# A scheduler's DMA model, the pace of attention against the FFN, and the place of one load in a fused attention and FFN kernel

## The chip, the core and the metric

The kernel runs on one core of a Trainium2 chip. Its time is the device time of one execution in microseconds (us). The core has a matrix engine (PE, whose weight loads are listed as PEld), a vector engine (DVE), a scalar engine (ACT), a general engine (POOL) and a queue engine (SP). DMAs are issued from SP and from POOL, on a queue each, and their bytes go through 16 DMA engines that both share.

## What is computed

```python
scores = scale * np.matmul(q, k.transpose(0, 1, 3, 2))     # q, k, v: 8 x 12 x 448 x 64
scores = np.einsum('bhij,hg->bgij', scores, w_pre)          # w_pre, w_post: 12 x 12
attn = np.exp(scores - np.max(scores, axis=-1, keepdims=True))
attn = attn / (np.sum(attn, axis=-1, keepdims=True) + 1e-09)
attn = np.einsum('bhij,hg->bgij', attn, w_post)
x = np.matmul(attn, v).transpose(0, 2, 1, 3).reshape(3584, 768)
h = np.maximum(x @ w_in, 0.0)                               # w_in: 768 x 2048
out = (h * h) @ w_out                                       # w_out: 2048 x 768
```

This is attention in which the 12 heads are mixed before and after the softmax ("talking heads"), and behind it an FFN with a squared ReLU.

## The kernel before

**The work of one batch.** There are eight batches. For each, T (L491, `tr`) turns q and k on PE into `qkt`; a head pair is a unit, and a batch has six. QK (L544, `qk`) makes the scores of 120 query rows and one head pair, in four row tiles of six pairs; the scores are copied to `stage` by ACT or DVE (`sev`). One DMA on SP's queue, called a move here (`rel`, L591), then lays ten query rows of all twelve heads from `stage` into a slot of `dring` (12 slots), so that heads stand on the partitions: 45 such chunks to a batch, 360 in all. `pre` (L619) mixes the heads of a chunk with one matmul, ACT takes the exponentials and their sums (L627), DVE the reciprocal (L637), POOL folds it into the second mixing matrix (`wk2s`, L643), and `post` (L675, four matmuls) mixes again. The result is copied to `a2t` (`a2ev`). AV (L737) multiplies it by v into `xt`, F1 (L796) makes 16 tiles of h, which ACT or DVE rectifies (L824, L825) and POOL squares (L834; DVE in the last batch), and F2 (L878) makes the output, which POOL's queue stores (L924).

**What has to wait for what.** A `pre` waits for its move. A move waits for all six copies of its row tile, and for the `pre` of twelve chunks earlier, whose slot it takes. AV of a half of a batch waits for its 23 or 22 chunks. F1 of a batch waits for AV of that part, and F2 of a batch for all its squares; F1 of the next batch comes behind F2 of this one. The loads are issued on POOL's queue: q and k of batch b + 1 when the last T of batch b is done, v of batch b + 1 when the last AV of batch b is done. At the start q and k of batch 0 come first, then the four pieces of `w_in`, then v of batch 0, q and k of batch 1, and `w_out`.

**The order.** All engines run a fixed order that a planner in Python (`_Plan`) writes when the kernel is built. It keeps a clock for each engine with assumed durations. PE's work is in seven streams (T, QK, pre, post, AV, F1, F2), each in its own order; `_pick` takes the next unit from the head of one of them. Among the heads that it believes ready with a margin to spare (`MARGIN`, and `MARGIN_DMA` for a `pre`, which waits for a move) it takes the one of the lowest priority number: AV 1, post 2, pre 3, QK 4, T 5, F1 and F2 5.5 to 7. The copies of ACT and DVE (`FLEX`) go to the engine that is free first by its clocks. When a DMA lands is assumed in `_commit`: loads queue behind each other (`load_free`) at the rate `LOAD`; a move that starts while loads are under way is itself delayed, and moves the end of the loads still to be issued by 500 ns. The planner only writes the order; on the chip each engine waits by semaphores for the real events.

F1 of a batch is done for all 448 columns at once, but in the batches in `split` part by part (four parts in batch 0, two halves in others).

Of the kernel before, what the change touches and what calls it, by code (L numbers as in the profile page):

```python
# [18 lines left out]
MODE_SWITCH = 100.0  # L19
ACT_BIAS = 50.0  # L20
MARGIN = 250.0
MARGIN_DMA = 1200.0
INF = float("inf")


class _Sem:
    __slots__ = ("handle", "count", "name")

    def __init__(self, handle, name):
        self.handle = handle  # L30
        self.count = 0
        self.name = name
# [31 lines left out]
class _Unit:  # L64


    __slots__ = ("prio", "mode", "nbanks", "needs", "go", "dma", "hold")

    def __init__(self, prio, go, needs, nbanks=0, mode=None, dma=False, hold=False):
        self.prio = prio  # L70
        self.go = go
        self.needs = needs
        self.nbanks = nbanks
        self.mode = mode
        self.dma = dma
        self.hold = hold


class _Plan:

    def __init__(self, nbanks):
        self.tasks = []
        self.ready = []
        self.free = {e: 0.0 for e in ENGINE_NAMES}
        self.per_engine = {e: [] for e in ENGINE_NAMES}
        self.committed = []
        self.streams = []
        self.mode = None
        self.load_free = 0.0
        self.move_free = 0.0  # L90
        self.bank_users = {i: [] for i in range(nbanks)}
        self.bank_age = {i: i for i in range(nbanks)}
        self.taken = set()
        self.age = nbanks

    def add(self, name, engine, fn, deps=(), cost=None, prio=0.0, sem=None, seminc=0,
            mode=None, after=(), dma=None):
# [21 lines left out]
    def _commit(self, t, e, start):  # L119
        t.engine = e  # L120
        held, lat = t.cost[e]
        self.free[e] = start + held
        t.end = start + lat
        if t.dma:
            kind, service = t.dma
            if kind == "load":
                self.load_free = max(self.load_free, start + 1200.0) + service
                t.end = max(start + held, self.load_free) + 1600.0
            else:
                at = start + 900.0  # L130
                behind = self.load_free - at
                if behind > 0:
                    at += min(behind, 2600.0)
                    service += 600.0
                    self.load_free += 500.0
                self.move_free = max(self.move_free, at) + service
                t.end = self.move_free + 2100.0
        t.done = True
        self.per_engine[e].append(t)
        self.committed.append(t)  # L140
        for s in t.succs:
            s.nwait -= 1
# [36 lines left out]
    def _pick(self):  # L179


        now = self.free[PE]
        found = []
        for s in self.streams:
            u = s[0] if s else None
            if u is None:
                continue
            needs = u.needs()
            if needs is None:
                continue  # L190
# [12 lines left out]
        if not found:  # L203
            return None
        first = min(f[0] for f in found)
        sure = [f for f in found if f[1] <= first + 1.0]
        if sure:
            def rank(f):
                u = f[2]
                p = u.prio  # L210
                if u.mode is not None:
                    if u.mode == self.mode:
                        p = min(p, 0.5)
                    elif u.hold and self.free_banks(first) < 4:
                        p += 10.0
                return (p, f[0])
            f = min(sure, key=rank)
        else:
            f = min(found, key=lambda f: (f[0], f[2].prio))
        return f  # L220
# [30 lines left out]
def bass_talking_heads_attention__then__ffn_squared_relu_kernel(  # L251
# [10 lines left out]
    B, H, S, D = q.shape  # L262
# [16 lines left out]
    NG = B * NCH  # L279
    scale = 1.0 / math.sqrt(D)  # L280

    with ExitStack() as es:
# [9 lines left out]
        NOS = 3  # L292
        NH1 = 3
        NWP = 4
        WC = 256
        ident = sb("ident", [128, 128], DT.bfloat16)
        mask = sb("mask", [NR, CH], DT.float32)
# [32 lines left out]
        sem_v = Sm("dv")  # L330
# [4 lines left out]
        plan = _Plan(NB)  # L335
# [73 lines left out]
        def rows(t, b, h0, nh):  # L409
            return bass.AP(t, (b * H + h0) * S * D, [[RJ * D, JB], [S * D, nh], [1, RJ * D]])  # L410

        LOAD = 1.0 / 350.0
        qk_tasks = {}
        v_of = {}

        def emit_load_qk(b):
            step = 4 if b == 0 else H
            for h0 in range(0, H, step):
                sem = sem_qk[h0 // step]

                def fn(eng, en, b=b, h0=h0, step=step, sem=sem):
                    eng.dma_start(qraw[:, h0:h0 + step, :, :],  # L422
                                  rows(q.tensor, b, h0, step)).then_inc(sem.handle, 16)
                    eng.dma_start(kraw[:, h0:h0 + step, :, :],
                                  rows(k.tensor, b, h0, step)).then_inc(sem.handle, 16)

                t = plan.add("ldqk%d_%d" % (b, h0), POOL, fn, [last.get("T")],
                             {POOL: (1400.0 if b == 0 else 2000.0, 0.0)},
                             -1e7 + h0 if b == 0 else b * 1000.0 - 1500.0, sem, 32,
                             dma=("load", 2 * step * S * D * 4 * LOAD))  # L430
                for h in range(h0, h0 + step):
                    qk_tasks[(b, h)] = t
            last["ldqk"] = t

        def emit_load_v(b):
            def fn(eng, en, b=b):
                eng.dma_start(vraw[:, :, :, :], rows(v.tensor, b, 0, H)).then_inc(
                    sem_v.handle, 16)

            last["v"] = v_of[b] = plan.add(  # L440
                "ldv%d" % b, POOL, fn, [last.get("AV")], {POOL: (1000.0, 0.0)},
                -1e5 if b == 0 else b * 1000.0 - 1600.0, sem_v, 16,
                dma=("load", H * S * D * 4 * LOAD))

        def emit_load_w(i, after=()):
# [160 lines left out]
        def unit_pre(g):  # L606
            b, c = divmod(g, NCH)
# [43 lines left out]
                    rel_wait.remove(g + NDS)  # L651
                    emit_rel(g + NDS)

            return _Unit(3.0, go, needs, 1, dma=True)

        av_of = {}

        def unit_post(g):
# [36 lines left out]
                a2_of[g] = t_a2  # L695
                give([bank], [t_a2])

            return _Unit(2.0, go, needs, 1)

        FIRST = ((0, 13), (13, HC[0]), (HC[0], 34), (34, NCH))  # L700

# [5 lines left out]

        xtev = {}
        f1_of = {}
        split = (0, B - 1)  # L710

        def unit_AV(b, part):
            half = 0 if part[0] < HC[0] else 1
# [221 lines left out]
        for b in range(B):  # L935
# [11 lines left out]
            for tile in tiles_of(b):  # L947
                for hh in range(2):
                    s_F2 += units_F2(b, tile, hh)

        emit_load_qk(0)
        emit_load_w(0)
        emit_load_v(0)
# [95 lines left out]
```

## Time and profile before

| | |
|---|---|
| median of 3 runs | 644.42 us (638.36 to 649.12) |
| profiled execution | 646.08 us, of which 644.3 us are the span of its instructions |
| mean granted PE clock | 0.957 |
| PE | busy 586.8 us (91%), 5864 matmuls |
| ACT, DVE, POOL | busy 450.4, 341.4, 311.2 us |
| moves (SP's queue) | 360, 38.56 MB |
| loads, stores (POOL's queue) | 33.82 MB |

The page lists busy time and idle time by engine and by groups of instructions, and the chain of work that ended last: from the last instruction back, at each step to what released it. Its rows name a line of the kernel and the tiles written and read (`out<-in`). Other views give the same by stretches of time, waits by pairs, and a timeline.

### The profile page before, as it was taken

What the parts mean: (1) busy time and instruction counts of PE and PEld (TensorE: products, weight loads), DVE (VectorE), ACT (ScalarE), POOL (GpSimd) and SP (SyncE); (2) the same over time, 40 slices, a digit from 0 to 9 for tenths busy, and PEclk for the clock granted to TensorE, in tenths of its full rate; (3) what the DMA queues carried; (4) which work ended last, traced back from release to release, by engine and by line L of the source; (5) the groups of instructions that cost most, each with busy time, mean ns of one, the idle gap of its engine ahead of it and who ended that gap; (6) DMA issues with size and microseconds to landing.
All of it is one profiled execution on the core that took longest, in us unless ns stands there. A gap on an engine that the chain in (4) does not pass through costs nothing.

```text
span 644.3 us, 15422 instructions
## 1 busy us (share of the span) xinstructions
PE 586.8 (91%) x5864; PEld 381.9 (59%) x5864; DVE 341.4 (53%) x854; ACT 450.4 (70%) x1163; POOL 311.2 (48%) x634
## 2 busy tenths in 40 slices
PE   4584999997999898979997999999999999999995
PEld 3243778665566555536654376655765476656973
DVE  3362988675677576643776337870674557300410
ACT  2571987995888787757887578965898688652531
POOL 8831768334483534545436444537446534571001
PEclk9775999998999999979999899999999999999998
DMA  9999959849752974482738636450635455301002
GB/s 138 217 229 170 172 120 167 157 113 152 131 115 51 177 164 115 84 166 44 154 83 146 120 40 153 108 145 5 117 97 117 89 104 127 94 1 48 28 25 73
DMA packets 95180, 73.36 MB, mean 114 GB/s; under 512 B 5508, under 2 KB 93060, under 8 KB 95108
## 3 DMA queue, kind: packets, MB, share of 16 engines
q0 software_dynamic: 48256, 33.82, 32.9%
q1 hardware_dynamic: 46852, 38.56, 25.9%
q8 instruction: 47, 0.77, 0.5%
q14 instruction: 25, 0.20, 0.1%
HBM read 45.62 MB, written 11.01 MB: 88 GB/s over the span
## 4 chain that ended last, share of the span: by engine, by line
PE 76%; DMA 16%; POOL 2%; SPq 2%; ACT 1%; DVE 1%; issue 1%; POOLq 0%; ACTq 0%
PE ps L878 21%; PE ps L796 20%; PE ps L675 11%; DMA dring<-stage 9%; PE ps L619 9%; DMA kraw<-in_k_dram 7%; PE ps L737 6%; PE ps L544 6%; PE ps L491 3%; SPq L591 2%; DVE stage L353 1%; POOL h2t L834 1%; POOL qraw L422 1%; POOL wk2s L643 1%; ACT stage L352 0%
## 5 line engine op out<-in xcount | busy, mean ns | idle before, releaser
L627 ACT ACTIVATE pring<-ps 120x448 bf16<-120x448 f32 x360 | 192.5, 554 | 38.2 <-PE ps L619 36.9
L643 POOL TENSOR_SCALAR wk2s<-wk2b,rinv 120x120 bf16<-120x120 bf16 x360 | 128.7, 364 | 142.4 <-DVE rinv L637 140.3
L353 DVE CAST a2t<-ps 112x480 bf16<-112x480 f32 x215 | 136.7, 649 | 87.9 <-PE ps L675 86.7
L878 PE MATMUL ps<-w_out_sb,h2t 128*128 128x384 bf16 x896 | 170.8, 326 | 0.0
L796 PE MATMUL ps<-xt,w_in_sb 128*128 128x448 bf16 (+6 forms) x1152 | 170.1, 294 | 0.0
L619 PE MATMUL ps<-dring,wk 120*120 120x448 bf16 x360 | 118.8, 372 | 25.5 <-DMA dring<-stage 24.8
L834 POOL TENSOR_TENSOR h2t<-h1t 128x448 bf16<-128x448 bf16 (+4 forms) x160 | 112.0, 707 | 53.2 <-ACT h1t L824 20.7
L796 PEld LDWEIGHTS ps<-xt,w_in_sb 128*128 128x128 bf16 x1152 | 95.0, 99 | 54.2 <-issue 8.4
L675 PE MATMUL ps<-wk2s,pring 120*128 120x120 bf16 x1440 | 121.2, 221 | 2.0 <-ACT stage L352 0.9
L675 PEld LDWEIGHTS ps<-wk2s,pring 120*128 120x128 bf16 x1440 | 95.6, 100 | 40.9 <-issue 9.4
L353 DVE CAST stage<-ps 120x896 bf16<-120x896 f32 (+1 forms) x95 | 102.2, 1084 | 26.9 <-PE ps L544 25.6
L878 PEld LDWEIGHTS ps<-w_out_sb,h2t 128*128 128x128 bf16 x896 | 83.9, 98 | 54.4 <-issue 4.7
L352 ACT ACTIVATE stage<-ps 120x896 bf16<-120x896 f32 (+1 forms) x97 | 86.2, 917 | 23.1 <-PE ps L544 21.8
L352 ACT ACTIVATE a2t<-ps 112x480 bf16<-112x480 f32 x145 | 80.8, 573 | 21.0 <-PE ps L675 20.0
L824 ACT ACTIVATE h1t<-ps 128x448 bf16<-128x448 f32 (+6 forms) x121 | 53.3, 445 | 40.7 <-PE ps L796 39.4
L637 DVE RECIPROCAL rinv<-rowsum 120x1 f32<-120x1 f32 x360 | 52.0, 155 | 54.7 <-ACT pring L627 53.5
L627 ACT ACTIVATION_READ_ACCUMULATOR pring<-ps 120x1 f32 x360 | 78.1, 217 | 0.0
L924 POOL DMA_DIRECT2D out_dram<-osb x56 | 30.5, 546 | 86.3 <-ACT osb L352 62.3
L619 PEld LDWEIGHTS ps<-dring,wk 120*120 120x120 bf16 x360 | 45.6, 137 | 44.0 <-DMA dring<-stage 14.0
L544 PE MATMUL ps<-qkt 64*120 64x448 bf16 (+1 forms) x384 | 60.3, 385 | 2.8 <-DVE stage L353 2.0
L825 DVE TENSOR_SCALAR h1t<-ps 128x448 bf16<-128x448 f32 (+5 forms) x71 | 28.8, 410 | 60.6 <-PE ps L796 57.7
L737 PE MATMUL ps<-a2t,vraw 112*64 112x230 bf16 (+5 forms) x864 | 41.6, 257 | 0.6 <-DVE rinv L637 0.6
(31 smaller groups left out, 272.4 us busy)
## 6 DMA issues: line engine op xcount, KB each, us to landing
dring<-stage SPq DMA_DIRECT2D x352, 105.0 KB
vraw<-in_v_dram POOLq DMA_DIRECT2D x8, 672.0 KB, 8.0
qraw<-in_q_dram POOLq DMA_DIRECT2D x7, 672.0 KB, 11.8
kraw<-in_k_dram POOLq DMA_DIRECT2D x7, 672.0 KB, 17.2
w_in_sb<-in_moe_w_in_dram POOLq DMA_DIRECT2D x8, 384.0 KB, 13.0
w_out_sb<-in_moe_w_out_dram POOLq DMA_DIRECT2D x12, 256.0 KB, 42.4
out_dram<-osb POOLq DMA_DIRECT2D x8, 336.0 KB, 3.7
out_dram<-osb POOLq DMA_DIRECT2D x8, 288.0 KB, 2.8
```

The source lines that it names most:

```text
L352: return eng.activation(o, i_, AF.Copy)
L353: return eng.tensor_copy(o, i_)
L544: r_ = eng.matmul(ps[0:nr, banks[par], 0:S], qkt[r0:r0 + 64, pb, p, 0, T * IT:T * IT + nr], qkt[r0:r0 + 64, pb, p, 1, :], start=True, stop ...
L619: return eng.matmul(ps[0:NR, bank, 0:S], wk1[:, :, :], dring[:, slot, :], start=True, stop=True)
L627: return eng.activation(pring[:, pr, 0:S], ps[0:NR, bank, 0:S], AF.Exp, accum_out=rowsum[:, pr, :])
L643: return eng.tensor_scalar(wk2s[:, ws, :], wk2b[:, :, :].rearrange("p a b -> p (a b)"), rinv[:, pr, :], 1.0, op0=ALU.mult, op1=ALU.mult)
L675: r_ = eng.matmul(ps[0:128, bank, jb * NR:(jb + 1) * NR], pring[:, pr, jb * JB:jb * JB + 128], wk2s[:, ws, :], start=True, stop=True,)
L737: r_ = eng.matmul(ps[kk * 64:kk * 64 + 64, bank, x * n:(x + 1) * n], vraw[:, h, r, :], a2t[half][:, r, h, a0:a0 + n], start=(r == 0), stop ...
L796: r_ = eng.matmul(ps[:, bank, 0:n], w_in_sb[:, ft, t16 * 128:(t16 + 1) * 128], xt[:, ft, c0:c1], start=(ft == 0), stop=(ft == NFT - 1),)
L824: return eng.activation(h1t[:, s, 0:n], ps[:, bank, 0:n], AF.Relu)
L834: return eng.tensor_tensor(h2t[:, t16, o0:o0 + n], h1t[:, s, 0:n], h1t[:, s, 0:n], ALU.mult)
L878: r_ = eng.matmul(ps[:, bank, 0:FH], h2t[:, t16, col:col + 128], w_out_sb[:, t16, hh * FH:(hh + 1) * FH], start=(t16 == 0), stop=(t16 == N ...
```

## The change

It has six edits, all in what the planner assumes or is told; no engine instruction has another shape but those of F1 of batch 1.

1. A move that is issued while loads are under way now delays every load that is not yet believed landed, by 520 ns (`STEAL`), and not only loads still to come.
2. The assumed rate of the loads is 385 and not 350 bytes a nanosecond.
3. A `pre` is believed sure only when its move is expected to have landed 3 us earlier (`MARGIN_DMA`), before 1.2 us.
4. `ahead` holds attention back: when more than 60 chunks plus the share of the FFN already done (times 360) have been posted, `pre` and `post` get 5 added to their priority number, and come behind T and F1, and level with F2 or behind it.
5. v of batch 0 is issued behind the first piece of `w_in` and not behind the fourth.
6. F1 of batch 1 is done in two halves.

```diff
-MARGIN_DMA = 1200.0
+MARGIN_DMA = 3000.0
+STEAL = 520.0
...
@@ _Plan._commit
             if kind == "load":
                 self.load_free = max(self.load_free, start + 1200.0) + service
                 t.end = max(start + held, self.load_free) + 1600.0
+                self.loads.append(t)
             else:
                 at = start + 900.0
                 behind = self.load_free - at
                 if behind > 0:
                     at += min(behind, 2600.0)
                     service += 600.0
-                    self.load_free += 500.0
+                    self.load_free += STEAL
+                    self.loads = [x for x in self.loads if x.end > max(at, self.move_free)]
+                    for x in self.loads:
+                        x.end += STEAL
                 self.move_free = max(self.move_free, at) + service
                 t.end = self.move_free + 2100.0
...
@@ _Plan._pick
         if sure:
+            late = self.ahead()
+
             def rank(f):
                 u = f[2]
                 p = u.prio
+                if late and u.paced:
+                    p += 5.0
...
-        LOAD = 1.0 / 350.0
+        LOAD = 1.0 / 385.0
...
@@ emit_load_v (VPOS = 0.5)
-                -1e5 if b == 0 else b * 1000.0 - 1600.0, sem_v, 16,
+                -2e5 + VPOS if b == 0 else b * 1000.0 - 1600.0, sem_v, 16,
...
-            return _Unit(3.0, go, needs, 1, dma=True)
+            return _Unit(3.0, go, needs, 1, dma=True, paced=True)
...
-            return _Unit(2.0, go, needs, 1)
+            return _Unit(2.0, go, needs, 1, paced=True)
...
-        split = (0, B - 1)
+        split = (0, 1, B - 1)
...
+        f_all = [len(s_F1), len(s_F2)]
+
+        def ahead():
+            done = (f_all[0] - len(s_F1)) / f_all[0] + (f_all[1] - len(s_F2)) / f_all[1]
+            return NG - len(s_post) > LEAD + NG * done / 2
+
+        plan.ahead = ahead
```

The lines of the changed kernel are numbered 15 higher in this part: T is L506, QK L559, `pre` L634, `post` L690, AV L752, F1 L811, F2 L893.

**The first place is on PE, near the start**, where T of batch 1 (the rows with `ident`) stands. Before, it comes behind three tiles of F1 of the first part of batch 0 (130 columns, six matmuls a tile):

```order
L675 MATMUL ps<-wk2s,pring 128x120 x12
L619 MATMUL ps<-dring,wk 120x448
L675 MATMUL ps<-wk2s,pring 128x120 x4
L796 MATMUL ps<-xt,w_in_sb 128x130 x12
L619 MATMUL ps<-dring,wk 120x448
L796 MATMUL ps<-xt,w_in_sb 128x130 x6
L491 MATMUL ps<-ident,qraw 64x112 x8
L491 MATMUL ps<-ident,kraw 64x112 x8
```

In the changed kernel the same place goes on with F1, QK, `pre` and `post` of batch 0; its T of batch 1 comes only behind these rows, the last of a stretch that begins at the same `pre`:

```order
L634 MATMUL ps<-dring,wk 120x448 x4
L690 MATMUL ps<-wk2s,pring 128x120 x4
L634 MATMUL ps<-dring,wk 120x448
L752 MATMUL ps<-a2t,vraw 64x100 x48
L690 MATMUL ps<-wk2s,pring 128x120 x20
L811 MATMUL ps<-xt,w_in_sb 128x100 x21
L690 MATMUL ps<-wk2s,pring 128x120 x4
L811 MATMUL ps<-xt,w_in_sb 128x100 x3
L506 MATMUL ps<-ident,qraw 64x112 x8
L506 MATMUL ps<-ident,kraw 64x112 x8
```

Between that `pre` (chunk 18 of batch 0) and T of batch 1 there stood 6 matmuls of F1 (of the 18 shown, 12 stand ahead of the `pre`); now there are 96 of 130 columns and 24 of 100, 12 of QK, 12 `pre`, 56 of `post` and 48 of AV.

**The second place is on PE, where batch 2 begins.** Before, the last rows of T of batch 3 (which let POOL issue the loads of q and k of batch 4) stand two rows above this piece, and the second matmul of the row `x2` that ends it is `pre` of chunk 5 of batch 2:

```order
L878 MATMUL ps<-w_out_sb,h2t 128x384 x4
L675 MATMUL ps<-wk2s,pring 128x120 x4
L619 MATMUL ps<-dring,wk 120x448
L544 MATMUL ps<-qkt 120x448 x2
L619 MATMUL ps<-dring,wk 120x448 x2
L878 MATMUL ps<-w_out_sb,h2t 128x384 x4
L675 MATMUL ps<-wk2s,pring 128x120 x8
L619 MATMUL ps<-dring,wk 120x448
L675 MATMUL ps<-wk2s,pring 128x120 x4
L619 MATMUL ps<-dring,wk 120x448
L878 MATMUL ps<-w_out_sb,h2t 128x384 x4
L619 MATMUL ps<-dring,wk 120x448 x2
```

In the changed kernel T of batch 3 is followed by chunks 24 and on of batch 1, six `pre` in a row among them:

```order
L506 MATMUL ps<-ident,qraw 64x112 x8
L506 MATMUL ps<-ident,kraw 64x112 x8
L690 MATMUL ps<-wk2s,pring 128x120 x8
L634 MATMUL ps<-dring,wk 120x448 x6
L893 MATMUL ps<-w_out_sb,h2t 128x384 x8
L690 MATMUL ps<-wk2s,pring 128x120 x4
L634 MATMUL ps<-dring,wk 120x448
L690 MATMUL ps<-wk2s,pring 128x120 x4
L634 MATMUL ps<-dring,wk 120x448
```

T of batch 3 has moved ahead by some 16 chunks, and the loads that it releases with it; F1 of batch 1 stands between it and batch 2.

**The third place is on POOL, at the start**, with the queue of loads. Before:

```order
L459 DMA w_in_sb<-in_moe_w_in_dram 128x6x256 x2
L377 AFFINE_SELECT mask<-mask 120x10
L459 DMA w_in_sb<-in_moe_w_in_dram 128x6x256 x4
L437 DMA vraw<-in_v_dram 112x12x256
L422 DMA qraw<-in_q_dram 112x12x256
```

In the changed kernel:

```order
L452 DMA vraw<-in_v_dram 112x12x256
L392 AFFINE_SELECT mask<-mask 120x10
L474 DMA w_in_sb<-in_moe_w_in_dram 128x6x256 x6
L437 DMA qraw<-in_q_dram 112x12x256
L439 DMA kraw<-in_k_dram 112x12x256
```

v has passed three pieces of `w_in` (six DMAs); what comes behind it is as before.

More of the change, by code (lines that the diff above doesn't have):

```diff
@@ L64, with __init__ @@
 class _Unit:
-    __slots__ = ("prio", "mode", "nbanks", "needs", "go", "dma", "hold")
-    def __init__(self, prio, go, needs, nbanks=0, mode=None, dma=False, hold=False):
+    __slots__ = ("prio", "mode", "nbanks", "needs", "go", "dma", "hold", "paced")
+    def __init__(self, prio, go, needs, nbanks=0, mode=None, dma=False, hold=False,
+                 paced=False):
+        self.paced = paced
         self.prio = prio
@@ L90, in __init__ @@
         self.move_free = 0.0
+        self.loads = []
         self.bank_users = {i: [] for i in range(nbanks)}
@@ L94, in __init__ @@
         self.age = nbanks
+        self.ahead = lambda: False
     def add(self, name, engine, fn, deps=(), cost=None, prio=0.0, sem=None, seminc=0,
@@ L294, in bass_talking_heads_attention__then__ffn_squared_relu_kernel @@
         NWP = 4
+        LEAD = 60
+        VPOS = 0.5
         WC = 256
```

## The prediction

> **What bounds the kernel now.** I read the page first: the busy shares, the slices in time and the granted clock.
>
> ```profile
> PE 586.8 (91%) x5864; PEld 381.9 (59%) x5864; DVE 341.4 (53%) x854; ACT 450.4 (70%) x1163; POOL 311.2 (48%) x634
> PE   4584999997999898979997999999999999999995
> PEclk9775999998999999979999899999999999999998
> PE 76%; DMA 16%; POOL 2%; SPq 2%; ACT 1%; DVE 1%; issue 1%; POOLq 0%; ACTq 0%
> ```
>
> PE is the bound: it is busy 586.8 of 644.3 us, and idle 57.5 us. A 9 in its slices is 90% or more, so the idle time sits in the first four slices (16 us each) and in a few dents in the middle; the granted clock drops in the same slices. In the chain of work that ended last, DMAs hold 16%. The waits of PE say which:
>
> ```profile
> PE ps L619 <- DMA dring<-stage: 24.8, 18, 4.9
> PE ps L491 <- DMA kraw<-in_k_dram: 11.5, 2, 10.7
> PE ps L491 <- POOL ident L363: 8.2, 1, 8.2
> ```
>
> Columns: us in total, times, the longest. `pre` waits for moves, and T for the load of k, once for 10.7 us. The third row is the start of the program, which nothing here touches; these three are 44.5 of the 57.5 us, and 7 more are the last store. Then the busy time by stretches (us, busy time of PE, PEld, DVE, ACT, POOL with their instructions, then the granted clock, the DMA engines' share and GB/s):
>
> ```profile
> 19.40:46.90 27.50, 19.50 (x167) 11.46 (x165) 13.52 (x36) 18.01 (x50) 13.67 (x29) 0.69 1.35 226
> 46.90:57.80 10.90, 0.21 (x6) 0.07 (x4) 0.46 (x2) 0.51 (x2) 1.77 (x5) 0.65 1.19 203
> 57.80:63.80 6.00, 6.00 (x106) 5.68 (x107) 3.51 (x6) 1.50 (x3) 0.89 (x1) 0.50 0.92 125
> 63.80:140.00 76.20, 75.23 (x1131) 56.36 (x1130) 60.98 (x170) 66.77 (x193) 46.98 (x129) 1.00 0.82 146
> 140.00:360.00 220.00, 200.39 (x1949) 124.73 (x1948) 133.94 (x325) 169.79 (x443) 106.30 (x215) 0.96 0.64 123
> 360.00:560.00 200.00, 198.76 (x1793) 123.83 (x1792) 112.09 (x273) 156.94 (x402) 101.82 (x199) 1.00 0.45 99
> 560.00:637.30 77.30, 77.25 (x606) 53.60 (x603) 9.20 (x33) 29.41 (x67) 22.34 (x30) 1.00 0.12 37
> ```
>
> Two places are worth anything: the 10.7 us before T of batch 1 (46.9 to 57.8), and 19.6 us (220.00 less 200.39) between 140 and 360. From 360 to the last matmul PE idles 1.3 us in 277; the last 77 us are F1 and F2 alone, and PE fills them. The chain in order of time shows what the waits in the middle are (start, us, what):
>
> ```profile
> 16.95 40.68 DMA kraw<-in_k_dram
> 148.49 8.29 DMA dring<-stage
> 268.67 9.52 DMA dring<-stage
> 347.13 8.31 DMA dring<-stage
> 494.66 3.90 DMA dring<-stage
> ```
>
> A move takes 3.9 us from issue to landing when it runs alone (the row at 494.66) and 8.3 to 9.5 us in the three that held PE up. What ran beside them is on POOL's timeline:
>
> ```profile
> 148.23 1.00 POOL L422 DMA_DIRECT2D qraw<-in_q_dram  x1
> 149.23 0.95 POOL L424 DMA_DIRECT2D kraw<-in_k_dram  x1
> ```
>
> The load of q and k goes out at 148.23, the move that PE will wait for at 148.49. So the stalls are collisions: a row tile's moves start together with a load, and the `pre` that needs them stands too close behind.
>
> **The start.** k of batch 1 is issued at 16.95 and lands at 57.63. PE comes to T at 46.9, with nothing else in its order. The new order puts a block in between, from the counts under the first order rows:
>
> ```profile
> L796 PE MATMUL ps<-xt,w_in_sb 128*128 128x130 bf16 x96 | 7.4, 220 | 0.0
> L796 PE MATMUL ps<-xt,w_in_sb 128*128 128x100 bf16 x96 | 6.0, 208 | 0.0
> L544 PE MATMUL ps<-qkt 64*88 64x448 bf16 x96 | 15.2, 371 | 0.0
> L737 PE MATMUL ps<-a2t,vraw 112*64 112x100 bf16 x48 | 1.3, 208 | 0.0
> 304.90 1.37 PE ps L675 x24
> 306.27 1.14 PE ps L619 x6
> ```
>
> Matmuls overlap, so a price is busy time by count and not the mean: 96 of F1 at 130 columns 7.4 us; 24 at 100 columns a quarter of 6.0, 1.5; 12 of QK an eighth of 15.2, 1.9; 48 of AV 1.3; 56 of `post` at 57 ns (1.37 by 24) 3.2; 12 `pre` at 0.19 (1.14 by 6) 2.3. That is 17.6 us. From 46.6 (the end of the `pre` of chunk 18, 0.3 us ahead of the stall) PE comes to T at 64.2, behind the landing at 57.63. So the wait of 10.7 us should go; what is late next is the copies. They are 12 exponentials with the reading of their sum, 14 copies to `a2t`, 6 to `stage` and 20 ReLUs:
>
> ```profile
> L627 ACT ACTIVATE pring<-ps 120x448 bf16<-120x448 f32 x360 | 192.5, 554 | 38.2 <-PE ps L619 36.9
> L627 ACT ACTIVATION_READ_ACCUMULATOR pring<-ps 120x1 f32 x360 | 78.1, 217 | 0.0
> L353 DVE CAST a2t<-ps 112x480 bf16<-112x480 f32 x215 | 136.7, 649 | 87.9 <-PE ps L675 86.7
> L352 ACT ACTIVATE stage<-ps 120x896 bf16<-120x896 f32 (+1 forms) x97 | 86.2, 917 | 23.1 <-PE ps L544 21.8
> L825 DVE TENSOR_SCALAR h1t<-ps 128x130 bf16<-128x130 f32 x11 | 3.1, 285 | 0.8 <-PE ps L796 0.5
> ```
>
> At these means (ns) that is 9.3 + 9.1 + 5.5 + 5.7 = 29.6 us for ACT and DVE together, 14.8 each if they share evenly: under 17.6, but not by much, so I leave 2 us for waits on them. The wait also cost clock: 57.80 to 63.80 ran at 0.50, half of 6.0 us, 3.0. If PE works through 46.9 to 64, the half clock has no idle stretch to follow. Sum for the start: 10.7 + 3.0 - 2 = **11.7 us gained**, with ends of 6 (the first rival) and 13.7.
>
> v of batch 0, moved ahead of three pieces of `w_in`, I cost at nothing: AV of the first part needs thirteen chunks, whose moves come in from 19.4 to 46.9, a stretch that the loads fill (DMA share 1.35) and that stays. The pieces of `w_in` that v passes land later by its 1.4 MB, some 6 us at 226 GB/s; the last of them is needed by tiles 12 to 15 of F1, deep in the block above. If that cover failed it would cost those 6 us at most.
>
> **The middle.** At the second place PE had 5.5 us of matmuls, by the same prices, between the last T of batch 3 and the `pre` of chunk 5 of batch 2, and the move took 8.3. Now 26 us stand between the two. I counted the same for every chunk: the PE work from the event that releases its move to its `pre`. Beside the five loads of q and k from batch 3 on the least was 3.1 to 5.0 us in four cases of the old order; in the new one it is 8.9 to 10 us, but for 7.2 at the last of them, and 5.7 and 5.9 us beside two loads of v. Loads of q and k make 8.3 to 9.5 (rows above); beside a load of v no row of the chain stands, and I bound it by 3.9 and 8.3 and take 6, nearer to the lone move since v has half their bytes. So three places may still wait, by up to 1 us each. I remove the 19.6 us and put 3 back. The stalls' clock goes with them:
>
> ```profile
> 350.90:353.90 3.00, 0.09 (x3) 0.02 (x1) 0.79 (x3) 0.90 (x2) 1.61 (x3) 1.00 1.30 186
> 353.90:360.70 6.80, 5.72 (x18) 2.12 (x18) 1.48 (x5) 2.80 (x7) 0.76 (x1) 0.50 0.99 180
> 156.90:162.80 5.90, 5.89 (x58) 5.12 (x59) 1.47 (x5) 1.52 (x4) 0.82 (x3) 0.50 1.04 203
> 278.30:282.20 3.90, 3.87 (x17) 2.09 (x18) 1.38 (x5) 1.27 (x4) 1.41 (x3) 0.50 0.95 176
> ```
>
> Behind the three stalls PE worked 5.72, 5.89 and 3.87 us at 0.50; half of 15.5 is 7.7 us. Sum for the middle: 19.6 + 7.7 - 3 = **24.3 us gained**, with ends of 0 (the waits come back under later loads) and 27.3.
>
> [...]
>
> **Pace and halves.** Holding `pre` and `post` back puts F1 and F2 beside them and moves the end of attention some 33 us of PE work later, into the stretch from 560 on where ACT and DVE stood nearly idle. In itself this moves nothing on a full PE: 0, with a cost only if what is left behind attention no longer hides its copies (the rival below). Halving F1 of batch 1:
>
> ```profile
> 559.45 18.16 PE ps L796 x96
> L796 PE MATMUL ps<-xt,w_in_sb 128*128 128x230 bf16 x96 | 9.6, 262 | 0.0
> L796 PE MATMUL ps<-xt,w_in_sb 128*128 128x218 bf16 x96 | 9.1, 257 | 0.0
> ```
>
> 9.6 + 9.1 against 18.16 is 0.5 us more. Its 16 more squares and ReLUs lie on POOL (48% busy) and on ACT or DVE beside PE; without that cover they would cost a few us.
>
> **The sum.** 646.08 of the profiled execution, less 11.7, less 24.3, plus 0.5, is 610.6. Of the 1.2 us that PE idles from 360 to 560 I take 1, since the moves there get the same longer lead: the forecast is **609.6 us**. The profiled execution stands 1.7 us above the median of the three runs, 644.42, whose own spread is 10.8 us; I make no correction.
>
> **The rivals.**
>
> *The start gives back half.* The moves of chunks 31 to 42 (twelve, as many as `dring` has slots) now go out while k of batch 1 is still on its way, and take from its time.
>
> ```profile
> dring<-stage SPq DMA_DIRECT2D x352, 105.0 KB
> ```
>
> At the 226 GB/s of the first stretch one is 0.47 us, twelve 5.6, and k lands at 63.2, still ahead of T; at twice that price it lands at 68.8, T waits 4.6 us, and some of the half clock comes back, 6 us in all. For it: loads and moves visibly slow each other (8.3 us against 3.9). Against it: moves queue beside this load in the old run too. Time: 609.6 + 6 = 615.6. [...]
>
> *The collisions move instead of going.* Every load of q and k still has to meet some moves, and by the count the margin is 1 to 2 us. If half the middle comes back: 609.6 + 12.2 = 621.8; if all of it, that is, if the change does not do what its model says: 633.9.
>
> *Bursts of `pre` choke ACT, and it gets slower.* Held back, attention comes in lumps: the new order has 24 runs of four to six `pre` in a row, the old one 10. Six hold six of the eight PSUM banks until ACT has done six exponentials, six times 0.554 + 0.217 or 4.6 us. If PE stood through all of it in the 14 new runs it would cost 65 us: 674. It turns to slower, over 657, once a run costs 3.4 us. Against it: the old order has five of its runs from 360 on, where PE idles 1.3 us in all.
>
> **How the numbers follow.** The forecast 0.64 (602 to 618); half the start back 0.10 (615.6); the middle half back 0.15 (618 to 633, a quarter of that over 631.5); all of it back 0.05 (633 to 640); bursts 0.03 (674); better than 602, 0.03. About 2% (13 us) is what a measurement of this kernel can tell from no change, so faster means below 631.5: 0.64 + 0.10 + 0.11 + 0.03 = 0.88. Within 2%: 0.04 + 0.05 = 0.09. Slower: 0.03. The range goes down to 599: the sum with 13.7, 27.3 and 1.2 taken whole is 604.4, less half the runs' spread. It goes up to 628: the forecast with half the middle and 6 us of the start given back. It leaves out about 0.02 below and 0.14 above.
>
> **What the profile of the changed kernel would show.** Start: T's row in PE's waits for k falls from 11.5 to below 2 us, and the stretch from 46 to 64 shows PE busy over 14 us at clock 1.00. Middle: `pre` waits for `dring` under 8 us in all (24.8 now, of which the first stretch keeps some 6), and no 0.50 between 100 and 560. Pace: exponentials run until some 45 us before PE's end, against 78. I would be wrong if k of batch 1 lands well after 64, if moves beside loads take over 10 us, or if PE's idle time reappears ahead of F1 or `post` with ACT as the releaser.

## The result and the profile after

The changed kernel takes **621.82 us** (median of 4 runs, 619.96 to 625.03), against 644.1 us for the kernel before beside it: a ratio of 0.9688, with an interval of 0.9602 to 0.9774. A second set of runs, beside its own runs of the kernel before, gave 618.44 us and 0.9577 (0.9529 to 0.9625). Here and below, medians are over all runs of a kernel, while ratios and intervals leave out single slow runs, over 1.5% above the fastest of their kernel (one of the kernel before here, and one each with the margin at 1.2, without the pace and with the margin at 4). The forecast was 609.6 us with a range of 599 to 628: faster as foreseen, inside the range, but by some two thirds of the gain. The profiled execution took 620.22 us, 25.9 less than before and not 36.5.

The page of the changed kernel: busy time, PE in its 40 slices (now 15.5 us each), the granted clock, and the chain by engine.

```profile
PE 580.8 (94%) x5960; PEld 389.1 (63%) x5960; DVE 340.8 (55%) x870; ACT 454.0 (73%) x1163; POOL 314.5 (51%) x650
PE   3589999999799989999989999999999999999995
PEclk9779999999799989999989999999999999999998
PE 83%; DMA 11%; POOL 2%; DVE 2%; issue 1%; ACT 1%; SPq 1%; POOLq 0%; DVEq 0%
```

The low digits of the fourth slice are gone, and in the middle three dents remain, the 7 of the eleventh slice and the 8 of the fifteenth and the twenty-first, and the clock has the same digits there. DMAs hold 11% of the chain, 16% before. PE's waits, in the same columns as before (us in total, times, longest):

```profile
PE ps L634 <- DMA dring<-stage: 14.2, 12, 4.4
PE ps L506 <- POOL ident L378: 8.2, 1, 8.2
PE ps L634 <- DVE stage L368: 2.9, 3, 1.4
...
PE ps L506 <- DMA kraw<-in_k_dram: 1.2, 1, 1.2
```

T's wait for k fell from 11.5 to 1.2 us, and what is left is T of batch 0 at 11.14 us: T of batch 1 doesn't wait. `pre`'s wait for moves fell from 24.8 to 14.2, not below 8. By stretches of time (busy us of PE, PEld, DVE, ACT, POOL, then clock, DMA share, GB/s):

```profile
46.90:64.00 17.10, 16.48 (x300) 13.23 (x299) 14.79 (x46) 13.59 (x39) 12.17 (x34) 1.00 1.07 192
64.00:80.00 16.00, 16.00 (x290) 13.07 (x284) 13.88 (x47) 14.19 (x42) 12.58 (x34) 1.00 1.10 173
80.00:140.00 60.00, 58.57 (x803) 42.43 (x800) 43.48 (x113) 47.09 (x121) 32.90 (x80) 1.00 0.90 169
140.00:360.00 220.00, 210.49 (x2127) 138.54 (x2125) 138.62 (x334) 178.32 (x464) 115.57 (x234) 0.97 0.60 119
360.00:560.00 200.00, 199.80 (x1749) 125.97 (x1747) 100.29 (x254) 153.86 (x393) 103.71 (x199) 1.00 0.44 95
```

The start works: 16.48 of 17.1 us busy at full clock. The middle still loses 220.00 less 210.49, 9.5 us, where before it lost 19.6. From 360 on PE stands for 0.2 us in 200.

**What is left in the middle** is seen on PE's timeline (start, duration, instruction, and in brackets the idle time before it and what ended it) at the two largest stops:

```profile
159.14 0.37 PE L690 MATMUL ps<-wk2s,pring 120*128 120x120 bf16 x4
162.46 0.37 PE L634 MATMUL ps<-dring,wk 120*120 120x448 bf16 x1 [2.94 <-DMA dring<-stage]
...
221.41 0.38 PE L690 MATMUL ps<-wk2s,pring 120*128 120x120 bf16 x4
224.16 0.37 PE L634 MATMUL ps<-dring,wk 120*120 120x448 bf16 x1 [2.37 <-DMA dring<-stage]
```

The chain has the moves (start, us from issue to landing), and POOL's timeline what was issued beside them:

```profile
154.77 9.44 DMA dring<-stage
214.47 9.54 DMA dring<-stage
311.13 8.12 DMA dring<-stage
```

```profile
153.60 1.01 POOL L452 DMA_DIRECT2D vraw<-in_v_dram  x1 [0.98 <-PE ps L752]
215.10 0.97 POOL L452 DMA_DIRECT2D vraw<-in_v_dram  x1 [0.93 <-PE ps L690]
310.09 1.01 POOL L437 DMA_DIRECT2D qraw<-in_q_dram  x1 [1.72 <-PE ps L506]
```

Each of the three lies within 1.2 us of a load: of v of batch 2, v of batch 3, and q and k of batch 7. The prediction had counted the least lead beside two loads of v and the last load of q and k, and these three fit it. The clock went with them:

```profile
163.50:170.30 6.80, 5.95 (x41) 5.19 (x42) 2.29 (x8) 2.60 (x7) 2.38 (x6) 0.50 0.31 97
225.00:228.40 3.40, 3.40 (x16) 1.52 (x14) 1.66 (x4) 2.21 (x6) 0.45 (x2) 0.51 0.67 206
320.50:323.90 3.40, 3.40 (x17) 1.63 (x16) 1.88 (x4) 1.89 (x3) 0.90 (x3) 0.50 0.81 157
```

12.75 us of matmuls at half clock, a loss of 6.4 us; before it was 7.7.

### The profile page after: what moved, and what is told of

Its sections match the earlier page's. It is cut to its first block, busy times and chain, and to the rows that moved or that the text cites. A ratio compares the mean times of both kernels' runs of the same rounds, so it can differ in the third digit from the quotient of the medians.

```text
span 618.5 us, 15729 instructions
## 1 busy us (share of the span) xinstructions
PE 580.8 (94%) x5960; PEld 389.1 (63%) x5960; DVE 340.8 (55%) x870; ACT 454.0 (73%) x1163; POOL 314.5 (51%) x650
## 4 chain that ended last, share of the span: by engine, by line
PE 83%; DMA 11%; POOL 2%; DVE 2%; issue 1%; ACT 1%; SPq 1%; POOLq 0%; DVEq 0%
PE ps L893 23%; PE ps L811 22%; PE ps L690 11%; DMA dring<-stage 10%; PE ps L634 10%; PE ps L559 7%; PE ps L752 6%; PE ps L506 3%; DMA kraw<-in_k_dram 1%; DVE stage L368 1%; POOL wk2s L658 1%; SPq L606 1%; POOL h2t L849 0%; POOL qraw L437 0%; DVE a2t L368 0%
## 5 line engine op out<-in xcount | busy, mean ns | idle before, releaser
L811 PE MATMUL ps<-xt,w_in_sb 128*128 128x448 bf16 (+6 forms) x1248 | 175.4, 283 | 0.0
L893 PE MATMUL ps<-w_out_sb,h2t 128*128 128x384 bf16 x896 | 170.5, 328 | 0.2 <-POOL h2t L849 0.2
L368 DVE CAST a2t<-ps 112x480 bf16<-112x480 f32 x206 | 130.8, 649 | 71.2 <-PE ps L690 68.8
L849 POOL TENSOR_TENSOR h2t<-h1t 128x448 bf16<-128x448 bf16 (+6 forms) x176 | 114.5, 662 | 48.0 <-DVE h1t L840 24.8
L811 PEld LDWEIGHTS ps<-xt,w_in_sb 128*128 128x128 bf16 x1248 | 102.5, 99 | 44.1 <-issue 6.1
L634 PE MATMUL ps<-dring,wk 120*120 120x448 bf16 x360 | 109.5, 366 | 17.3 <-DMA dring<-stage 14.2
L690 PE MATMUL ps<-wk2s,pring 120*128 120x120 bf16 x1440 | 121.9, 220 | 1.8 <-POOL wk2s L658 1.5
L690 PEld LDWEIGHTS ps<-wk2s,pring 120*128 120x128 bf16 x1440 | 97.2, 100 | 41.3 <-POOL wk2s L658 5.1
L893 PEld LDWEIGHTS ps<-w_out_sb,h2t 128*128 128x128 bf16 x896 | 83.3, 98 | 55.7 <-issue 8.1
L368 DVE CAST stage<-ps 120x896 bf16<-120x896 f32 (+1 forms) x90 | 97.2, 1086 | 29.5 <-PE ps L559 24.2
L367 ACT ACTIVATE a2t<-ps 112x480 bf16<-112x480 f32 x154 | 85.9, 574 | 22.0 <-PE ps L690 20.6
L367 ACT ACTIVATE stage<-ps 120x896 bf16<-120x896 f32 (+1 forms) x102 | 91.0, 916 | 10.1 <-PE ps L559 7.0
L634 PEld LDWEIGHTS ps<-dring,wk 120*120 120x120 bf16 x360 | 45.9, 135 | 36.8 <-DMA dring<-stage 11.7
L839 ACT ACTIVATE h1t<-ps 128x448 bf16<-128x448 f32 (+6 forms) x99 | 44.2, 449 | 26.9 <-PE ps L811 26.1
L559 PE MATMUL ps<-qkt 64*120 64x448 bf16 (+1 forms) x384 | 60.4, 390 | 1.8 <-DVE stage L368 0.9
L840 DVE TENSOR_SCALAR h1t<-ps 128x448 bf16<-128x448 f32 (+6 forms) x109 | 41.8, 388 | 25.2 <-PE ps L811 22.7
L367 ACT ACTIVATE osb<-ps 128x384 f32<-128x384 f32 x36 | 17.7, 491 | 40.1 <-PE ps L893 39.8
```

The lines of the kernel that those rows point to most:

```text
L367: return eng.activation(o, i_, AF.Copy)
L368: return eng.tensor_copy(o, i_)
L559: r_ = eng.matmul(ps[0:nr, banks[par], 0:S], qkt[r0:r0 + 64, pb, p, 0, T * IT:T * IT + nr], qkt[r0:r0 + 64, pb, p, 1, :], start=True, stop ...
L634: return eng.matmul(ps[0:NR, bank, 0:S], wk1[:, :, :], dring[:, slot, :], start=True, stop=True)
L690: r_ = eng.matmul(ps[0:128, bank, jb * NR:(jb + 1) * NR], pring[:, pr, jb * JB:jb * JB + 128], wk2s[:, ws, :], start=True, stop=True,)
L811: r_ = eng.matmul(ps[:, bank, 0:n], w_in_sb[:, ft, t16 * 128:(t16 + 1) * 128], xt[:, ft, c0:c1], start=(ft == 0), stop=(ft == NFT - 1),)
```

## The experiments

**Were the two loads of v the missing gain?** The order of all engines stays as in the changed kernel, but the loads of v of batches 2 and 3 bring one head of twelve (so the kernel leaves out most of v of these batches):

```diff
+                nh = 1 if b in (2, 3) else H
-                eng.dma_start(vraw[:, :, :, :], rows(v.tensor, b, 0, H)).then_inc(
+                eng.dma_start(vraw[:, 0:nh, :, :], rows(v.tensor, b, 0, nh)).then_inc(
```

> The changed kernel with its order untouched; only the loads of v of batches 2 and 3 are cut to one head of twelve, which leaves out most of v of these two batches. Theory (the waits left in the middle are moves held up by the loads of v): the waits of pre at 159.5 to 164.4 (2.9 and 1.0 us) and at 221.8 (2.4 us) go, and the half clock behind them, 6.8 and 3.4 us of it, with them; 6.3 + 5.1 = 11 us less, about 611. Rival A (the moves are late by each other, or PE would wait for something else there): the waits stay, within 3 us of the changed kernel. Rival B (the loads of v delay the moves, but the clock halves for another reason): the waits go and the half clock stays, 6 us less, about 616.

Measured: 612.45 us, 0.9475 (0.9429 to 0.952). The two stretches around the loads, first in the changed kernel, then with the loads cut:

```profile
153.00:172.00 19.00, 15.03 (x143) 12.42 (x138) 10.32 (x30) 11.31 (x34) 9.53 (x21) 0.82 0.57 113
212.00:232.00 20.00, 17.43 (x163) 11.16 (x162) 9.81 (x27) 14.38 (x42) 8.34 (x19) 0.91 0.74 160
```

```profile
153.00:172.00 19.00, 18.98 (x203) 15.01 (x202) 17.33 (x49) 18.06 (x54) 13.93 (x33) 1.00 0.41 85
212.00:232.00 20.00, 19.80 (x165) 12.29 (x164) 14.78 (x39) 18.08 (x52) 8.57 (x23) 1.00 0.57 133
140.00:360.00 220.00, 215.66 (x2210) 142.56 (x2208) 143.14 (x353) 184.75 (x486) 118.48 (x246) 0.98 0.60 121
```

Both stops are gone, and both drops of the clock with them. Nothing but these bytes was changed, so the two collisions are shown to be the cause of their stalls and of the half clock, together about 10 us by the profiles (620.22 less 610.28) and 6 to 9 by the medians. The stop at the third place stays: 2.6 of the 4.3 us that PE still idles in the middle.

**Edit 1 undone**, the rest of the change kept:

```diff
-STEAL = 520.0
+STEAL = 500.0
...
-                    self.loads = [x for x in self.loads if x.end > max(at, self.move_free)]
-                    for x in self.loads:
-                        x.end += STEAL
```

> The changed kernel without edit 1: a move delays only loads still to come, by 500 ns, as before. In its order T of batch 1 stands ahead of AV of the first part of batch 0, where PE comes at about 43 us, while k of batch 1 lands at 57 to 58. Theory (edit 1 makes the whole gain of the start): PE waits 14 us there again and runs at half clock behind it, 14 to 18 us more than the changed kernel, 636 to 640, with pre waiting for moves about as in the changed kernel after 100 us. Rival (the start is gained by the later pre or the later pieces of the order, not by the loads' assumed end): under 5 us more, below 627.

Measured: 630.05 us, 0.9764 (0.972 to 0.9809). PE's wait for k, and the stretches of the stall and behind it:

```profile
PE ps L503 <- DMA kraw<-in_k_dram: 11.8, 2, 10.7
```

```profile
45.20:55.90 10.70, 0.00 (x0) 0.02 (x1) 0.44 (x2) 0.00 (x0) 0.00 (x0) 0.62 1.29 219
55.90:61.30 5.40, 5.39 (x83) 4.83 (x85) 2.83 (x5) 1.67 (x4) 0.18 (x1) 0.50 0.92 126
140.00:360.00 220.00, 209.64 (x2174) 138.22 (x2172) 142.70 (x350) 182.30 (x470) 119.96 (x245) 0.98 0.65 127
```

The 10.7 us are back to the tenth, and half clock behind them (the other 1.0 us of the first row is T of batch 0). The total rose by less, 0.008 and 0.019 of the time before against the two sets of the changed kernel (5 and 12 us), which lies between what the two theories asked for. Part of the difference is the middle's clock: one stretch of half clock here, of 6.8 us, where the changed kernel has three with 13.6 us in all.

**Edit 1 alone**, on the kernel before:

> The kernel before with edit 1 alone. In its order T of batch 1 stands behind more work than PE has until k of batch 1 lands at 57 to 58. Theory A (edit 1 is worth the start, and the waits between 140 and 360 go through one of the other edits): the wait of 10.7 us for k goes, 10 to 13 us less than before, 632 to 636, and PE idles 15 us or more between 140 and 360. Theory B (the old order merely met the loads badly; any new order gains there): 18 us less or more, below 628, and PE idles 10 us or less there. Rival (with v of batch 0 still behind w_in, AV waits in v's place): PE idles 5 us or more between 43 and 64, 640 or more.

Measured: 638.07 us, 0.9858 (0.9809 to 0.9906), some 9 us less than before, and 2 us above what theory A asked for.

```profile
PE ps L625 <- DMA dring<-stage: 24.7, 22, 4.1
...
PE ps L497 <- DMA kraw<-in_k_dram: 1.6, 1, 1.6
```

```profile
140.00:360.00 220.00, 203.55 (x1932) 123.20 (x1933) 143.43 (x341) 172.51 (x440) 110.32 (x219) 0.98 0.62 121
```

T of batch 1's wait for k goes with this edit by itself (the 1.6 us are T of batch 0). `pre` waits for moves as long as before (24.7 against 24.8), and PE idles 16.5 us in the middle, so most of the middle's gain is not this edit's.

**The margin back at 1.2 us.** If the longer lead before a `pre` was what halved the middle's stalls, this should bring them back:

```diff
-MARGIN_DMA = 3000.0
+MARGIN_DMA = 1200.0
```

> The changed kernel with MARGIN_DMA at 1200 as before. Its start is the changed kernel's. Theory (the longer margin is what took PE's waits out of the middle): waits of pre for moves between 100 and 360 us come back, 10 us or more of idle time with the half clock behind them, 13 to 20 us more than the changed kernel, 635 to 642. Rival (the middle was gained by edit 1 and the pace): within 5 us of the changed kernel, 617 to 627.

Measured: 613.75 us, 0.9498 (0.9469 to 0.9527). My theory fell: it became faster.

```profile
PE   4589899999999999999999999999999999999995
PEclk9789999999999999999999999999999999999999
```

```profile
140.00:360.00 220.00, 215.05 (x2253) 141.83 (x2252) 145.82 (x355) 183.49 (x472) 122.04 (x246) 1.00 0.66 131
```

No dent is left in the middle, where PE stands for 5.0 us, and no stretch of half clock follows. Yet this is no rule either, as the next two show.

**Rate 350, with the margin of 3 us and with that of 1.2 us:**

```diff
-        LOAD = 1.0 / 385.0
+        LOAD = 1.0 / 350.0
```

> The changed kernel with the loads' assumed rate at 350 as before. Theory (the assumed rate only shifts where units fall; no gain hangs on it): within 8 us of the changed kernel, 613 to 630, with no wait for k at the start. Rival (a rate that is too slow made the old order place things wrongly): waits between 140 and 360 come back to 15 us or more, 630 or more.

Measured: 615.45 us, 0.9512 (0.9459 to 0.9564).

> The changed kernel with MARGIN_DMA at 1200 and the assumed rate at 350, both as before; beside the kernel with the rate alone (615.5 us). Theory M (the longer margin costs: it lumps what waits, and a stall of over 2 us brings half clock, while 1200 ns leaves many small waits that do not): 6 us less than with the rate alone, 607 to 612, no stall over 1.5 us and no half clock between 100 and 560. Theory R (every new plan merely redraws which moves meet which loads): anything from 608 to 630, with two or three stalls over 2 us as in the other plans.

Measured: 632.53 us, 0.982 (0.9752 to 0.9887). Both theories missed it, R by 2.5 us, with four stops of 2.6 to 3.1 us in the middle. By the medians, with the rate of 385 the short margin was better than the long one by 5 to 8 us; with the rate of 350 it is worse by 17. Each edit's sign depends on the other, so neither has a worth of its own that these runs could show.

**A model with more delay in it**, which should make the planner leave more lead at loads: first with a margin of 4 us and up to 3.6 us that a move can stand behind a load, then the second alone with a margin of 1.2.

```diff
-MARGIN_DMA = 3000.0
+MARGIN_DMA = 4000.0
...
-                    at += min(behind, 2600.0)
+                    at += min(behind, 3600.0)
```

> The changed kernel with a dearer move in the planner: a move beside loads starts up to 3600 ns late, not 2600, and a pre is sure 4000 ns behind its move, not 3000. The profile of the changed kernel has moves beside loads at 8.4 to 9.6 us; this model has them at about 7.7 with 4 us of margin. Theory (what is left in the middle is a move's price beside a load that the planner sets too low): PE idles 5 us or less between 140 and 360, without half clock there, 8 to 12 us less than the changed kernel, 609 to 614. Rival (the longer margin itself makes lumps, and the kernel with 1200 ns was faster for that): no gain, 618 to 628, with stalls of over 2 us again.

Measured: 625.69 us, 0.9636 (0.9557 to 0.9715).

> The changed kernel with MARGIN_DMA at 1200, and a move beside loads assumed to start up to 3600 ns late, not 2600: the dearer price without the margin. Theory M: 607 to 614, no stall over 1.5 us and no half clock between 100 and 560. Theory R: 608 to 630, with two or three stalls over 2 us.

Measured: 628.21 us, 0.9745 (0.9698 to 0.9793). A more careful model isn't a faster order: the middle's idle time is 12.3 and 14.9 us in these two, and the times are those of the rival and of theory R.

**v of batch 0 back behind the fourth piece of `w_in`:**

```diff
-                -2e5 + VPOS if b == 0 else b * 1000.0 - 1600.0, sem_v, 16,
+                -1e5 if b == 0 else b * 1000.0 - 1600.0, sem_v, 16,
```

> The changed kernel with v of batch 0 behind the fourth piece of w_in again, as before; its whole order from chunk 5 of batch 0 on is planned anew. Theory (v's place is worth nothing by itself): between 43 and 64 PE idles as little as in the changed kernel, under 3 us, and the total lies within 8 us of it either way, by where the moves meet the loads. Rival (v's place opens the way for AV and F1 in the start): PE idles 5 us or more between 43 and 64, or T of batch 1 waits.

Measured: 630.57 us, 0.9739 (0.9682 to 0.9796).

```profile
46.90:64.00 17.10, 16.41 (x287) 13.54 (x282) 13.96 (x44) 12.78 (x38) 10.57 (x30) 1.00 1.06 191
46.90:80.00 33.10, 30.04 (x522) 24.94 (x517) 24.68 (x79) 21.00 (x66) 19.65 (x57) 0.95 0.96 166
80.00:140.00 60.00, 56.58 (x777) 40.78 (x776) 41.69 (x103) 42.74 (x113) 30.25 (x75) 0.97 0.81 154
140.00:360.00 220.00, 205.36 (x2101) 134.79 (x2099) 147.93 (x359) 172.65 (x449) 117.49 (x240) 0.99 0.63 122
```

T's place is safe without this edit. The total is outside the 8 us that the theory allowed. Of the 9 us by which it is over the first set of the changed kernel, 4.4 are idle time between 46.9 and 140 (6.5 against 2.05) and 5.1 are in the middle. Of the 4.4, 2.4 are one stop at 74.53 us that waits for nothing that the profile shows ("issue"). Stops like it, between 65 and 68 us, are in the next two runs too, where v is ahead (first row: v back; then no pace, no halves), so nothing shows that it comes from v's place:

```profile
PE ps L690 <- issue: 2.4, 1, 2.4
...
PE ps L506 <- issue: 2.9, 1, 2.9
...
PE ps L506 <- issue: 2.3, 1, 2.3
```

Whether the rest is v's place or the order that was drawn again wasn't told apart.

**No pace, and no halves of F1 of batch 1:**

```diff
-        LEAD = 60
+        LEAD = 100000
```

> The changed kernel with LEAD so large that attention is never held back. Its order differs from the changed kernel's only from batch 5 on, beyond 400 us of the profile, where neither the kernel before nor the changed one has idle time on PE; attention ends earlier there. Theory (the pace is worth nothing): the same as the changed kernel within its noise, 619 to 625. Rival A (the pace spares ACT and DVE and is worth time): 5 us more or worse, with PE idle beyond 400. Rival B (its runs of six pre cost time): 3 us or more less, below 619.

Measured: 622.68 us, 0.9614 (0.956 to 0.9668): the time of the changed kernel. Its order has 12 runs of four or more `pre`, the changed one 24.

```diff
-        split = (0, 1, B - 1)
+        split = (0, B - 1)
```

> The changed kernel without edit 6: F1 of batch 1 in one piece. The order differs from chunk 33 of batch 1 on. Theory (halves give PE work for the start of batch 2 earlier): waits of over 2 us come back between 130 and 230, 5 us or more above the changed kernel, 627 or more. Rival (the halves are worth nothing but a new draw of the order): 612 to 627.

Measured: 616.42 us, 0.9563 (0.9523 to 0.9603), not above the changed kernel (0.9577 on the same chip). The halves bring nothing that shows.

**The changed kernel again**, to see whether its stalls are a matter of one execution:

> The changed kernel itself, for a comparison on the same chip as the three others: within 1% of its first median of 621.8, 616 to 628.

Measured: 618.44 us, 0.9577. PE stands for 10.2 us in the middle (9.5), at the same `pre`, of the same chunks: 2.39, 2.13 and 3.76 us at 161, 222 and 318.7. So the places are set by the order. One size isn't: the third is 1.7 us in the first profile. No pace says the same: its order is the changed kernel's up to 367 us, and it stops for 3.60, 3.07 and 2.10 us at these three `pre`.

The third stop has a route of its own. The profile puts it down to a copy to `stage`, and in the repeat that copy on DVE itself waits 4.00 us for a move:

```profile
317.55 1.09 DVE L368 CAST stage<-ps 120x896 bf16<-120x896 f32 x1 [4.00 <-DMA dring<-stage]
```

`stage` has two buffers, so a copy must wait until the moves that read its buffer two row tiles earlier have landed, and `pre` here waits for the PSUM bank that the copy reads. With the loads of v cut the same copy waits 2.82 us. Moves held up beside a load thus stop PE by this route as well. No run cut the load of q and k that stands beside it.

**All orders side by side.** Idle is PE's between 140 and 360; the last four rows stand apart for what is noted there:

| kernel | idle, us | profiled us |
|---|---|---|
| loads of v cut | 4.3 | 610.28 |
| margin 1.2 | 5.0 | 611.06 |
| no halves | 6.5 | 618.40 |
| rate 350 | 7.1 | 617.83 |
| changed | 9.5 | 620.22 |
| changed again | 10.2 | 620.86 |
| margin 4, 3.6 behind | 12.3 | 623.31 |
| v back | 14.6 | 630.68 |
| margin 1.2, 3.6 behind | 14.9 | 628.33 |
| margin 1.2, rate 350 | 16.1 | 629.26 |
| no pace (the longest of its four runs) | 10.5 | 628.86 |
| edit 1 undone (no gain at the start) | 10.4 | 630.21 |
| edit 1 alone (4.3 us idle from 360 to 560, too) | 16.5 | 637.88 |
| before (no gain at the start) | 19.6 | 646.08 |

Over the first ten rows (eight orders) a straight line gives 1.6 us of time for each us of idle, and misses none by more than 3.1 us. One reason for more than 1 is in the profile of the changed kernel: behind a stall come 3.4 or 6.8 us at half clock. No pace lies 7.1 us above the line: up to 367 us it runs the same order as the changed kernel, but it has the stop of 2.9 us before 67.6 us, and 2.7 us of idle time from 360 to 560. So a single profile of an order can be off by several us.

## Why the prediction was right or wrong

**The start: right, and for its reason.** T of batch 1 is reached at 62.42 us (64.2 foreseen):

```profile
62.42 0.39 PE L506 MATMUL ps<-ident,qraw 112*64 112x112 bf16 x8
```

From 46.9 to 140 PE stands for 2.05 us, and before for 11.65 (93.1 less 6.41 + 15.60 + 59.44): 9.6 us; the 3.0 us of half clock are gone as well; up to 46.9 it is busy 0.8 us less than before, but 2.7 us less of it at half clock (10.9 us in 23.5 to 33.8 and 37.2 to 40.7, against 13.6 in 22.9 to 40.0), so it does 0.5 us more. That is 13.1 against the 11.7 of the sum, and inside its ends of 6 and 13.7: of the 2 us set aside for waits on copies 1.1 came. Two experiments from both sides pin the wait to edit 1. k of batch 1, issued at 17.40, landed 39.2 us later at 56.6, not after 64.

**The middle: the step that failed is the term "three places may still wait, by up to 1 us each", the 3 us left over.** The places fit, the price did not. The working took 6 us for a move beside a load of v, between 3.9 and 8.3; the two that decided took 9.44 and 9.54, over the upper end. With 9.5 in place of 6, the working's own leads of 5.7 and 5.9 us would have given stops of some 3.7 us each, so it is this price that was mis-sized. PE stopped for 2.94 + 1.02 us at the first place, 2.37 at the second, and at the third 0.54, behind 1.16 that the profile puts down to a copy to `stage`, a route by which a late move stops PE that the prediction didn't have; with smaller waits, 9.5 us. And I had let the stalls' clock go as a whole, 7.7 us, when the stops that remain keep 6.4 of it. So the middle gave 10.1 + 1.3 = 11.4 us where 24.3 were forecast. The time lies inside the range because the range had room for half of the middle, not because the middle's working held. The argument that v has half the bytes of q and k was the wrong one: the moves beside v were as late as those beside q and k (9.44 and 9.54 us against 8.29 to 9.52 before). Six was no bad price everywhere: beside v of batch 4, issued at 283.33, the five moves from 284.6 to 287.9 took 5.2 to 6.2 us by their events. That load itself landed in 7.4 us (first row below: DMA issues from 284 to 288, KB each, us to landing), and v of batch 2 in 11.9 (second row: those from 153 to 163). What made the one a lighter meeting than the other wasn't told apart.

```profile
vraw<-in_v_dram POOLq DMA_DIRECT2D x1, 672.0 KB, 7.4
...
vraw<-in_v_dram POOLq DMA_DIRECT2D x1, 672.0 KB, 11.9
```

Two rows of the chain are a sign of their own:

```profile
47.56 10.86 DMA dring<-stage
104.87 10.35 DMA dring<-stage
```

Moves of over 10 us I had named as a sign of being wrong. They cost little where they are, since PE idles 2.05 us in all from 46.9 to 140: there the lead was long enough.

**The checks.** T's wait 1.2 (below 2 foreseen) and 16.48 us busy from 46.9 to 64 (over 14): right. `pre` waiting 14.2 (below 8) and no 0.50 from 100 to 560: wrong, three times. From 360 to 560 1.0 us gained, as taken. The last exponential runs at 563.2 and PE ends at 611.4, 48 us later (45 foreseen). The sum by these: 13.1 + 11.4 + 1.0, less 0.5 for the halves, is 25.0 of the 25.9 us measured; 0.9 stays without a place.

**The clock.** In the changed kernel's profile half clock followed the stop of 2.94 us and that of 2.37 us, and also the two of 1.16 and 0.54 us, close together, at the third place:

```profile
318.35 0.40 PE L634 MATMUL ps<-dring,wk 120*120 120x448 bf16 x1 [1.16 <-DVE stage L368]
319.30 0.40 PE L634 MATMUL ps<-dring,wk 120*120 120x448 bf16 x1 [0.54 <-DMA dring<-stage]
```

Full clock came back after 6.8, 3.4 and 3.4 us. But a stop of this size doesn't always bring half clock. With the margin at 4 and 3.6 behind, one of 2.93 us was followed by full clock:

```profile
155.01 0.37 PE L634 MATMUL ps<-dring,wk 120*120 120x448 bf16 x1 [2.93 <-DMA dring<-stage]
...
155.10:162.00 6.90, 6.70 (x72) 5.33 (x73) 5.79 (x15) 5.03 (x12) 4.45 (x10) 1.00 1.10 197
```

What tells the two apart wasn't tested.

**The rivals.** "The collisions move instead of going" was nearest, with its half at 621.8. It had 0.15, and it deserved more. What speaks for it now isn't that half the stalls stayed where they were, but that every new order draws its own: 5.0 to 16.1 us of idle time among plans that differ from the changed one by a number or two, against 19.6 in the old one. "The start gives back half" fell: T of batch 1 doesn't wait for k, which lands at 56.6 us (63.2 and later by that rival). "Bursts of `pre`" fell: 24 runs instead of 12 take the same time, and no wait on ACT is among PE's larger ones. Pace: nothing, as foreseen. v's place: nothing foreseen, and nothing shown; some 2 us of the idle time before 140 us stay possible.

**What stays open** is whether edits 2, 3 and 5 are worth something by themselves. All plans profiled have a better middle than the kernel before, but putting one of these numbers back moves the time up or down by up to some 12 us, and two put back at once don't add up (3 to 8 us less each, 11 to 14 more together). One plan each doesn't tell a worth from a draw, all the less as one plan alone, no pace, ran from 618.39 to 628.86 us. The best complete kernel found is the changed one with the margin at 1.2 us, 0.9498 (0.9469 to 0.9527) against 0.9577 (0.9529 to 0.9625) and 0.9688 (0.9602 to 0.9774): a good draw, not a better rule.

## What to carry to other kernels

Where a planner writes the order, count the lead in front of each wait under the new order, and price a collision by the worst row of a like one, not by the bytes; in these profiles 1 us of standing went with 1.6 us of time, the clock included. Count the copies that wait for a move, too, and not only its reader. Of a planner's number, judge the stage that it aims at (here the wait for k, which came and went with one edit) and leave the total to several plans, since any other plan draws new collisions. To price one collision, keep the order and shrink the one transfer.

## What the runs showed of the hardware

A move of 105 KB took 3.90 us where no load was under way (only other moves; the row at 494.66 in the kernel before), 9.44 and 9.54 us when issued within 1.2 us of a load of v, 5.2 to 6.2 us beside another load of v, and up to 10.86 us in the first 140 us; cutting the two loads of v to a twelfth took their two stalls away with no other edit (PE busy 18.98 of 19.0 and 19.80 of 20.0 us there, in the changed kernel 15.03 and 17.43). Half clock came after stops of 2.94, 2.37 and 1.16 + 0.54 us and lasted 6.8, 3.4 and 3.4 us; after one of 2.93 us in another order there was none. In the kernel with the margin of 1.2 us, where PE stands for 5.0 us in all between 140 and 360, there was none there either (clock 1.00), though a move issued at 207.55 took 11.64 us: from 212 to 232, a stretch in which it landed, PE stood for 0.83 us, so this late move cost little.
